# Attention's opening in another order: u first, head copies on ScalarE, both tables at once, the second unit turned in idle banks, diagonals by halves

## The chip, the cores and the metric

The kernel runs on one core of one Trainium2 chip. A core has five engines with an instruction queue each, which run side by side and wait for one another by semaphores: TensorE (PE, matrix products and transposes; its weight loads have a row of their own, PEld), VectorE (DVE), ScalarE (ACT), GpSimd (POOL) and SyncE (SP, which here only issues transfers). Every queue is worked off in order: an instruction that waits holds up all that stand behind it on its engine. Sixteen DMA engines move data between the memory and the core's SBUF. PE writes its results to PSUM[...].

The metric is the device time of one execution in microseconds (us); the time of a kernel is the median of its runs.

## The reference

Two stages follow each other. The first is a linear attention with decay (RWKV-5), for 4 batches, 8 heads, 768 steps and a head size of 48:

```python
for t in range(S):
    kt, vt, rt = (k[:, :, t], v[:, :, t], r[:, :, t])
    cur = np.einsum('bhd,bhe->bhde', u[None] * kt, vt)
    y[:, :, t] = np.einsum('bhd,bhde->bhe', rt, state + cur)
    state = w[None, :, :, None] * state + np.einsum('bhd,bhe->bhde', kt, vt)
```

Each head's state fades by `w` at every step; the step's own product of key and value enters the output with the factor `u` and the state with the factor 1. The output, laid out as 3072 tokens of 384 numbers, goes to the second stage, a mixture of 8 experts. A gate gives a score to every pair of token and expert; the pairs are taken in falling order of score until each expert has exactly 384 tokens, and each token goes through its expert, `relu(x @ w1[e]) @ w2[e]` with 1024 hidden numbers.

## The kernel before

**Units.** The attention (class `Mild`) is cut into 24 units, one for each batch and each chunk of 128 steps, chunk by chunk. Unit n has three loads of 192 KB, k, r and v, which SP issues in the order of need (`load`, L336); a buffer slot for k and r is used again five units later, one for v six units later. `start` issues the loads of k and r of units 0 to 4 and v of units 0 to 3; the loop of unit n issues k and r of unit n+5 and v of unit n+4.

**What is done for a unit.** `again` (L340) copies the first head of the second half (k and r) once more behind the last head, so that every pair of heads that is turned together can be read as 112 neighbouring columns. `turn` transposes k and r on PE, four transposes each (L456, L462), into PSUM tiles kT_ps and rT_ps and scales them on the way out with tables of powers of w: in unit 0 with small pieces of the table Q (L468), in units 1 and 2 with the tables WK and WR (L471, L474); from unit 3 on POOL scales the keys beforehand (`keys`, L431, with the table wk) and ACT copies kT out (L473). `own` computes r·k·u for every step on POOL (L437, L438), `own_sum` sums it by head on DVE into dd (L443), and `diagonal` writes eight matrices AT with dd on the diagonal on ACT (L484). `pairs` multiplies keys and r on PE into g_ps (L494), and DVE lays the upper part of it over AT (L498). `keep` forms the product of keys and values for the state (L511). `outputs` multiplies AT with v on PE (L532), and ACT copies the result x out (L550). `rows` transposes x back (L581), ACT copies it (L588), and SP writes it to memory (L589), from where the experts fetch their tokens.

**The order.** The order on each engine is written out by hand, by the order of the calls in `Mild.run`. In the loop of unit n, `turn` is two units ahead of `outputs` and `pairs` one. Ahead of the loop stands the opening, which the change rewrites:

```python
        self.start()
        self.again(0)
        self.turn(0, "pieces")
        self.own(0)
        self.idle(4, "y_ps")
        self.tables()
        self.wk_table()
        self.again(1)
        self.own_sum(0)
        self.diagonal(0)
        self.turn(1, "tables")
```

`start` also loads w and the row u_row (on ACT's queue, L360), makes the identity matrix, clears buffers, and computes the powers of w on DVE, then Q, half on POOL and half on DVE (L391). `spread_u` spreads u over the partitions by a product with a row of ones (u_ps, L406) and ACT copies it to u_bc (L407). `tables` copies WK and WR out of Q on ACT (L418). `wk_table` transposes WK on PE (L425), and ACT copies the result to wk (L426). `idle` issues transposes of the identity that nobody reads (L412). Inside `turn(0, "pieces")` the u product and three unread transposes stand between k's and r's transposes. u_ps, wk_ps, y_ps and the unread transposes share the PSUM tile with the tag y_ps.

**After the attention.** In the last units, pieces of the expert assignment are run between attention's steps. Then the experts follow one by one: a search for the next expert that fills, the fetch of its tokens by rows (POOL, indirect), its weights (SP), and the products. All of this is tied to attention's results and to the order on the engines, not to a point in time.

## Time and profile before

| | |
|---|---|
| median of 3 runs | 410.83 us (410.79 to 411.12) |
| the profiled execution | 411.54 us, of which the trace spans 409.8 |
| PE busy | 385.9 us |
| DVE, ACT, POOL busy | 274.0, 159.3, 140.5 us |
| PE's first product of unit 0 (L494) | at 15.30 us |
| the same of units 1, 2, 3, 4, 5 | at 18.60, 22.50, 28.05, 32.17, 36.29 us |
| loads k, r, v and writes of x_rows | 192 KB each; 3.0 to 5.3 us from issue to landing in the median |

Times are microseconds from the span's start. In a timeline line the first number is the start, the second the length from the first to the last of the merged instructions, then come engine, line, operation, output and inputs; in brackets stands for how long the engine was idle before it and whose result ended that. A name with q (SPq, ACTq) is the engine's queue, which issues transfers. In a line of the table of stretches the stretch is followed by its length, then by each engine's busy time with its number of instructions, the granted PE clock, the DMA engines' share and the rate.

### The profile page before, as it was taken

Reading aid. Unit: us, or ns where it says so; the run is one execution under the profiler, and the core shown is the slowest. Engines: PE = TensorE matmul, PEld = TensorE weight load, DVE = VectorE, ACT = ScalarE, POOL = GpSimd, SP = SyncE. Lnnn points to the kernel's source line nnn. Section 1 sums busy time; section 2 is a strip of 40 time slices with the busy share of each in tenths; the row PEclk is TensorE's granted clock in tenths of the full one; section 3 lists DMA queues with packets and bytes.
Section 4 is the critical chain, followed back from the end, with each engine's and each line's share of the span. In section 5 each row is a group of like instructions: output and inputs, shape, how many; then the busy total and the mean of one; then the engine's idle time right before and its main releaser. Section 6 shows DMA issues by size and latency. Waiting matters only on the chain.

```text
span 409.8 us, 8707 instructions
## 1 busy us (share of the span) xinstructions
PE 385.9 (94%) x3245; PEld 291.7 (71%) x3245; DVE 274.0 (67%) x951; ACT 159.3 (39%) x413; POOL 140.5 (34%) x172
## 2 busy tenths in 40 slices
PE   5899999999999897899999999999999999999993
PEld 3778888888877564558558757856856956966991
DVE  5776676566886789779487477568658852971630
ACT  1697888788873310222222221221312312132130
POOL 5697878566742021103403203202311222040020
PEclk9999999999999999999999999999999999999998
DMA  9999997988591263009219109108216365180010
GB/s 122 163 155 199 200 172 142 172 155 156 107 354 38 87 234 150 20 2 333 82 22 354 40 19 347 59 19 293 87 44 231 136 208 217 36 332 20 2 59 26
DMA packets 95301, 57.29 MB, mean 140 GB/s; under 512 B 77201, under 2 KB 89490, under 8 KB 95250
## 3 DMA queue, kind: packets, MB, share of 16 engines
q1 hardware_dynamic: 91520, 47.19, 46.5%
q0 software_dynamic: 3072, 9.44, 6.4%
q8 instruction: 27, 0.44, 0.5%
q14 instruction: 24, 0.20, 0.1%
q10 hardware_dynamic: 658, 0.01, 0.1%
HBM read 47.20 MB, written 9.44 MB: 138 GB/s over the span
## 4 chain that ended last, share of the span: by engine, by line
PE 63%; DVE 18%; DMA 11%; ACT 3%; issue 3%; POOLq 0%; ACTq 0%; DVEq 0%
PE h_ps L1494 18%; PE p_ps L1567 9%; DMA out_dram<-o_all,to 9%; PE y_ps L532 7%; PE o_ps L1594 6%; PE g_ps L494 5%; PE kv_ps L511 2%; PE kT_ps L456 2%; PE rT_ps L462 2%; PE x_ps L581 2%; PE lg_ps L561 2%; PE xT_ps L1485 2%; ACT AT L484 1%; DVE H L1545 1%; DMA xg<-x_rows,tok 1%
## 5 line engine op out<-in xcount | busy, mean ns | idle before, releaser
L1494 PE MATMUL h_ps<-xT,w 128*128 128x384 f32 (+1 forms) x384 | 122.5, 469 | 0.7 <-ACT xT L1486 0.6
L1494 PEld LDWEIGHTS h_ps<-xT,w 128*128 128x128 f32 x384 | 65.7, 190 | 37.0 <-issue 3.6
L1496 ACT ACTIVATE hid<-h_ps 128x384 f32<-128x384 f32 (+1 forms) x64 | 29.7, 464 | 93.7 <-PE h_ps L1494 88.4
L1470 POOL DMA_INDIRECT xg<-x_rows,tok x22 | 22.9, 1040 | 112.2 <-issue 69.6
L484 ACT ACTIVATE AT<-ident,dd 128x128 f32<-128x128 f32 x192 | 58.6, 390 | 1.2 <-DVE dd L443 1.2
L1588 POOL DMA_INDIRECT out_dram<-o_all,to x16 | 20.0, 1247 | 75.8 <-DVE o_all L1576 73.7
L498 DVE COPY_PREDICATED AT<-mask,g_ps 128x512 f32<-128x512 uint8 x48 | 32.7, 734 | 12.6 <-PE g_ps L494 12.3
L1571 ACT COPY res<-p_ps 128x384 f32<-128x384 f32 (+2 forms) x28 | 13.2, 473 | 59.0 <-PE p_ps L1567 59.0
L1594 PE MATMUL o_ps<-w,hid 128*128 128x384 f32 x96 | 32.8, 486 | 0.0
L494 PE MATMUL g_ps<-rT,kT 48*128 48x128 f32 x384 | 27.9, 285 | 0.6 <-DVE AT L498 0.6
L431 POOL TENSOR_TENSOR kss<-krs,wk 128x384 f32<-128x384 f32 x24 | 24.3, 1016 | 9.6 <-DVE krs L340 8.1
L494 PEld LDWEIGHTS g_ps<-rT,kT 48*128 48x128 f32 x384 | 23.3, 187 | 3.7 <-PE rT_ps L462 0.9
L438 POOL TENSOR_TENSOR rk<-rk,u_bc 128x384 f32<-128x384 f32 x24 | 24.2, 1008 | 4.6 <-ACT u_bc L407 2.8
L532 PE MATMUL y_ps<-AT,vts 128*64 128x128 f32 x384 | 25.7, 276 | 0.0
L437 POOL TENSOR_TENSOR rk<-krs 128x384 f32<-128x384 f32 x24 | 24.5, 1021 | 0.0
L1594 PEld LDWEIGHTS o_ps<-w,hid 128*128 128x128 f32 x96 | 17.4, 190 | 9.8
L532 PEld LDWEIGHTS y_ps<-AT,vts 128*64 128x64 f32 x384 | 20.6, 137 | 1.0 <-issue 0.3
L1567 PE MATMUL p_ps<-T,S 128*128 128x192 f32 x120 | 20.7, 327 | 0.0
L1545 DVE TENSOR_TENSOR H<-hid 128x512 f32<-128x512 f32 x12 | 7.9, 687 | 19.1 <-ACT hid L1496 19.1
L550 ACT COPY x<-y_ps 128x512 f32<-128x512 f32 x24 | 14.0, 584 | 16.0 <-PE y_ps L532 16.0
L1567 PEld LDWEIGHTS p_ps<-T,S 128*128 128x128 f32 x120 | 19.6, 190 | 0.0
L1567 PEld LDWEIGHTS p_ps<-w,hid 128*128 128x128 f32 x112 | 17.3, 190 | 1.9
(301 smaller groups left out, 691.6 us busy)
## 6 DMA issues: line engine op xcount, KB each, us to landing
w<-in_moe_w_dram SPq DMA_DIRECT2D x18, 1536.0 KB, 7.2
krs<-in_k_dram SPq DMA_DIRECT2D x24, 192.0 KB, 3.9
krs<-in_r_dram SPq DMA_DIRECT2D x24, 192.0 KB, 5.3
vts<-in_v_dram SPq DMA_DIRECT2D x24, 192.0 KB, 5.3
x_rows<-xr SPq DMA_DIRECT2D x24, 192.0 KB, 3.0
xg<-x_rows,tok POOLq DMA_INDIRECT x22, 4.5
out_dram<-o_all,to POOLq DMA_INDIRECT x16, 3.1
out_dram<-o_sb,to POOLq DMA_INDIRECT x5, 2.6
```

The source lines that it names most:

```text
L431: self.nc.gpsimd.tensor_mul(self.kss[:, n % self.NS].rearrange("p (g h) d -> p g h d", g=2)[:, :, :, 0:D], src, self.wk.rearrange("p (g h) ...
L437: nc.gpsimd.tensor_mul(rk, self.krs[:, n % self.NK, 1, 0:H, 0:D], self.krs[:, n % self.NK, 0, 0:H, 0:D])
L438: nc.gpsimd.tensor_mul(rk, rk, self.u_bc)
L484: nc.scalar.mul(AT[:, z, a, :], self.ident, dd[:, h:h + 1])
L494: nc.tensor.matmul(g_ps[:, z, a, :], kT[rows, a, :], rT[rows, a, :], start=True, stop=True)
L498: nc.vector.copy_predicated(out=AT[:, z], mask=self.mask.unsqueeze(1).to_broadcast([128, HP, T]), data=g_ps[:, z])
L532: nc.tensor.matmul(yv[q * PD:(q + 1) * PD, o // 2, o % 2, :], lhsT, rhs, start=(o // 2, q) not in seen, stop=stop, skip_group_check=True)
L1470: nc.gpsimd.indirect_dma_start(out=xg[:, c, :], out_offset=None, in_=x_dram[0:within, :], in_offset=bass.IndirectOffsetOnAxis(ap=tok[:, c: ...
L1494: nc.tensor.matmul(h_ps[:, 0:m], w1[:, f, ts(j, 128)], xT[:, f, 0:m], start=(f == 0), stop=(f == KD - 1))
L1496: nc.scalar.activation(hid[:, j, 0:m], h_ps[:, 0:m], AF.Relu)
L1567: nc.tensor.matmul(ps[:, q, :], left[a][:, j, :], right[b][:, j, :], start=(j == 0), stop=(j == KF // 2 - 1))
L1594: nc.tensor.matmul(o_ps, hid[:, j, ts(c, 128)], w2[:, j, :], start=(j == 0), stop=(j == KF - 1))
```

## The change

The opening's calls are put into another order, and some move to other engines.

- u_row is loaded from POOL's queue instead of ACT's. Its product comes first on PE, after 12 unread transposes instead of 14; the other unread transposes (3 and 4) are gone.
- `again` of units 0, 1 and 2 becomes two copies on ACT each (`again_one`, one for k and one for r), where it was one copy on DVE that waited for both loads. From unit 3 on it stays on DVE.
- k and r of unit 0 are turned one right after the other. Unit 1 is turned before the products of unit 0 as before, but into PSUM tiles of the assignment that stand idle at that time (tags few and counts), with WK's transposes between its k and r.
- WK and WR are made one after the other on ACT with `again_one` of unit 1 between; `chunk` comes later on DVE.
- `diagonal` goes by halves of the heads: all of z = 0, then all of z = 1. In unit 0 the copies for unit 2 stand between and behind the halves.
- `keys(0)` moves ahead of `pairs(0)` in the program.
- Units 3 to 23 and all that follows keep their code; only the order of the eight diagonals within a unit differs.

```diff
--- before.py
+++ after.py
@@ -339,6 +339,10 @@
         kr, HP, H, D = self.krs[:, n % self.NK], self.HP, self.H, self.D
         self.nc.vector.tensor_copy(kr[:, :, H, 0:D], kr[:, :, HP, 0:D])
 
+    def again_one(self, n, x):
+        t, HP, H, D = self.krs[:, n % self.NK, x], self.HP, self.H, self.D
+        self.nc.scalar.copy(t[:, H, 0:D], t[:, HP, 0:D])
+
     def start(self):
         nc, HP, H, D = self.nc, self.HP, self.H, self.D
         half = HP // 2
@@ -357,10 +361,10 @@
         AB = self.ones8
         nc.vector.memset(AB[:, :, :, :, 0:1], 1.0)
         nc.gpsimd.memset(self.wgp, 0.0)
-        nc.scalar.dma_start(self.u_row, self.u.rearrange("h d -> (h d)").unsqueeze(0))
+        nc.gpsimd.dma_start(self.u_row, self.u.rearrange("h d -> (h d)").unsqueeze(0))
         nc.vector.memset(self.one_row, 1.0)
         nc.scalar.copy(self.bad, self.ident[:, 0:HP])
-        self.idle(14, "y_ps")
+        self.idle(12, "g_ps")
 
         nc.gpsimd.memset(self.mask_f, 1.0)
         nc.gpsimd.affine_select(out=self.mask_f, in_=self.mask_f, compare_op=ALU.is_ge, fill=0.0, base=-1,
@@ -401,29 +405,30 @@
                                      self.wg.rearrange("(a z d) e -> z d a e", z=2, d=self.D)[z])
 
     def spread_u(self):
-        nc, H, D = self.nc, self.H, self.D
         u_ps = self.ps.tile([128, 512], F32, name="u_ps", tag="y_ps")
-        nc.tensor.matmul(u_ps[:, 0:H * D], self.one_row, self.u_row, start=True, stop=True)
-        nc.scalar.copy(self.u_bc.rearrange("p h d -> p (h d)"), u_ps[:, 0:H * D])
+        self.nc.tensor.matmul(u_ps[:, 0:self.H * self.D], self.one_row, self.u_row, start=True, stop=True)
+        return u_ps
+
+    def copy_u(self, u_ps):
+        self.nc.scalar.copy(self.u_bc.rearrange("p h d -> p (h d)"), u_ps[:, 0:self.H * self.D])
 
     def idle(self, m, tag):
         ps = self.ps.tile([128, 512], F32, name="unread_ps", tag=tag)
         for _ in range(m):
             self.nc.tensor.transpose(ps[:, 0:T], self.ident, self.ident)
 
-    def tables(self):
-        nc, AB = self.nc, self.ones8
-        for t, x in ((self.WK, "k"), (self.WR, "r")):
-            for at, q in self.pieces[x]:
-                nc.scalar.copy(t[:, :, at], q)
-        nc.vector.tensor_mul(self.chunk, AB[:, 0, :, 1, 8], AB[:, 0, :, 1, 8])
-
-    def wk_table(self):
-        nc, HP, D = self.nc, self.HP, self.D
+    def table(self, t, x):
+        for at, q in self.pieces[x]:
+            self.nc.scalar.copy(t[:, :, at], q)
+
+    def wk_turned(self):
         ps = self.ps.tile([128, 2, 512], F32, name="wk_ps", tag="y_ps")[:, 0].rearrange("p (a s) -> p a s", s=T)
-        for a in range(HP):
-            nc.tensor.transpose(ps[:, a, :], self.WK[:, a, :], self.ident)
-        nc.scalar.copy(self.wk, ps.rearrange("p a (z d) -> p (a z) d", z=2)[:, :, 0:D])
+        for a in range(self.HP):
+            self.nc.tensor.transpose(ps[:, a, :], self.WK[:, a, :], self.ident)
+        return ps
+
+    def wk_table(self, ps):
+        self.nc.scalar.copy(self.wk, ps.rearrange("p a (z d) -> p (a z) d", z=2)[:, :, 0:self.D])
 
     def keys(self, n):
         D = self.D
@@ -447,42 +452,46 @@
         s = 2 * a if t.shape[1] == self.H or 2 * a < self.HP else 2 * a + 1
         return t[:, s:s + 2, :].rearrange("p q d -> p (q d)")[:, 0:PD + self.D]
 
-    def turn(self, n, raw=None):
-        nc, HP, P = self.nc, self.HP, PD + self.D
-        kr = self.krs[:, n % self.NK]
-        key = self.kss[:, n % self.NS] if raw is None else kr[:, 0]
-        kT_ps = self.ps.tile([128, HP, T], F32, name="kT_ps")
-        for a in range(HP):
-            nc.tensor.transpose(kT_ps[0:P, a, :], self.pair(key, a), self.ident)
-        if raw == "pieces":
-            self.spread_u()
-            self.idle(3, "y_ps")
-        rT_ps = self.ps.tile([128, HP, T], F32, name="rT_ps")
-        for a in range(HP):
-            nc.tensor.transpose(rT_ps[0:P, a, :], self.pair(kr[:, 1], a), self.ident)
-        kT = self.pool.tile([128, HP, T], F32, name="kT")
-        rT = self.pool.tile([128, HP, T], F32, name="rT", bufs=3)
-        if raw == "pieces":
-            for t, t_ps, x in ((kT, kT_ps, "k"), (rT, rT_ps, "r")):
-                for at, q in self.pieces[x]:
-                    nc.vector.tensor_mul(t[0:P, :, at], t_ps[0:P, :, at], q[0:P])
+    def turned(self, n, t, pool, name, tag):
+        ps = pool.tile([128, self.HP, T], F32, name=name, tag=tag)
+        for a in range(self.HP):
+            self.nc.tensor.transpose(ps[0:PD + self.D, a, :], self.pair(t, a), self.ident)
+        return ps
+
+    def keys_turned(self, n, raw=False, pool=None, tag="kT_ps"):
+        key = self.krs[:, n % self.NK, 0] if raw else self.kss[:, n % self.NS]
+        return self.turned(n, key, pool or self.ps, "kT_ps", tag)
+
+    def r_turned(self, n, pool=None, tag="rT_ps"):
+        return self.turned(n, self.krs[:, n % self.NK, 1], pool or self.ps, "rT_ps", tag)
+
+    def scaled(self, n, x, ps, how):
+        nc, P = self.nc, PD + self.D
+        t = self.pool.tile([128, self.HP, T], F32, name=x + "T", bufs=2 if x == "k" else 3)
+        if how == "pieces":
+            for at, q in self.pieces[x]:
+                nc.vector.tensor_mul(t[0:P, :, at], ps[0:P, :, at], q[0:P])
+        elif how is None:
+            nc.scalar.copy(t[0:P], ps[0:P])
         else:
-            if raw:
-                nc.vector.tensor_mul(kT[0:P], kT_ps[0:P], self.WK[0:P])
-            else:
-                nc.scalar.copy(kT[0:P], kT_ps[0:P])
-            nc.vector.tensor_mul(rT[0:P], rT_ps[0:P], self.WR[0:P])
-        self.live[n].update(kT=kT, rT=rT)
-
-    def diagonal(self, n):
+            nc.vector.tensor_mul(t[0:P], ps[0:P], how[0:P])
+        self.live[n][x + "T"] = t
+
+    def turn(self, n, raw=False):
+        kT_ps = self.keys_turned(n, raw)
+        rT_ps = self.r_turned(n)
+        self.scaled(n, "k", kT_ps, self.WK if raw else None)
+        self.scaled(n, "r", rT_ps, self.WR)
+
+    def diagonal(self, n, zs=(0, 1)):
         nc, HP = self.nc, self.HP
-        AT = self.pool.tile([128, 2, HP, T], F32, name="AT", bufs=3)
-        dd = self.live[n]["dd"]
-        for a in range(HP):
-            for z in range(2):
+        if "AT" not in self.live[n]:
+            self.live[n]["AT"] = self.pool.tile([128, 2, HP, T], F32, name="AT", bufs=3)
+        AT, dd = self.live[n]["AT"], self.live[n]["dd"]
+        for z in zs:
+            for a in range(HP):
                 h = self.head(a, z)
                 nc.scalar.mul(AT[:, z, a, :], self.ident, dd[:, h:h + 1])
-        self.live[n]["AT"] = AT
 
     def pairs(self, n, between=None):
         nc, HP, D = self.nc, self.HP, self.D
@@ -604,22 +613,37 @@
         N, B, C, walk = self.N, self.B, self.C, self.walk
         self.live = {n: {} for n in range(N)}
         self.start()
-        self.again(0)
-        self.turn(0, "pieces")
+        u_ps = self.spread_u()
+        self.again_one(0, 0)
+        k0 = self.keys_turned(0, True)
+        self.again_one(0, 1)
+        r0 = self.r_turned(0)
+        self.copy_u(u_ps)
         self.own(0)
-        self.idle(4, "y_ps")
-        self.tables()
-        self.wk_table()
-        self.again(1)
+        self.scaled(0, "k", k0, "pieces")
+        self.scaled(0, "r", r0, "pieces")
+        self.table(self.WK, "k")
+        self.again_one(1, 0)
+        self.table(self.WR, "r")
+        self.again_one(1, 1)
+        k1 = self.keys_turned(1, True, walk.ps, "few")
+        wk_ps = self.wk_turned()
+        r1 = self.r_turned(1, walk.ps, "counts")
+        self.wk_table(wk_ps)
+        self.scaled(1, "k", k1, self.WK)
         self.own_sum(0)
-        self.diagonal(0)
-        self.turn(1, "tables")
+        self.diagonal(0, (0,))
+        self.again_one(2, 0)
+        self.diagonal(0, (1,))
+        self.again_one(2, 1)
+        self.scaled(1, "r", r1, self.WR)
         self.own(1)
+        self.keys(0)
         self.own_sum(1)
-        self.again(2)
+        nc, AB = self.nc, self.ones8
+        nc.vector.tensor_mul(self.chunk, AB[:, 0, :, 1, 8], AB[:, 0, :, 1, 8])
         self.pairs(0)
         self.diagonal(1)
-        self.keys(0)
         self.own(2)
         chores = walk.constants()
         for n in range(N):
@@ -628,7 +652,7 @@
             if n == 2:
                 self.gate_weights()
             if n == 0:
-                self.turn(2, "tables")
+                self.turn(2, True)
                 self.again(3)
                 self.own_sum(2)
                 self.pairs(1)
```

## Prediction

> **What bounds the kernel now.** I read the page first, then stretches of the opening, then each engine's timeline from 0 to 42 us, then the loads.
>
> ```profile
> span 409.8 us, 8707 instructions
> PE 385.9 (94%) x3245; PEld 291.7 (71%) x3245; DVE 274.0 (67%) x951; ACT 159.3 (39%) x413; POOL 140.5 (34%) x172
> PE 63%; DVE 18%; DMA 11%; ACT 3%; issue 3%; POOLq 0%; ACTq 0%; DVEq 0%
> ```
>
> PE is busy for 94% and carries most of the chain that ended last. It is idle for 23.9 us in all, so an opening can be worth a few us at most.
>
> ```profile
> 0.00:15.30 15.30, 10.60 (x43) 7.90 (x43) 7.76 (x24) 3.94 (x10) 8.72 (x19) 1.00 1.17 136
> 15.30:28.05 12.75, 11.07 (x145) 9.03 (x144) 10.66 (x21) 11.99 (x39) 10.86 (x12) 1.00 1.20 146
> 28.05:32.17 4.12, 4.12 (x64) 3.63 (x61) 3.09 (x7) 3.91 (x12) 3.84 (x5) 1.00 1.12 198
> ```
>
> The third stretch is one unit of the settled loop: PE has no gap in 4.12 us, and ACT fills 3.91. From 28 us on whatever PE has gained or lost stays. In the second stretch ACT is the full engine (11.99 of 12.75). So the question is where ACT and PE stand when that regime begins.
>
> ```profile
> 8.09 0.46 PE L456 MATMUL kT_ps<-ident,krs 128*112 128x128 f32 x1 [1.91 <-DVE krs L340]
> 8.48 1.64 PE L406 MATMUL u_ps<-u_row,one_row 1*128 1x384 f32 x2
> 15.30 1.16 PE L494 MATMUL g_ps<-rT,kT 48*128 48x128 f32 x16
> 26.91 0.61 PE L581 MATMUL x_ps<-ident,x 112*128 112x112 f32 x4 [0.68 <-ACT x L550]
> ...
> 14.91 4.78 ACT L484 ACTIVATE AT<-ident,dd 128x128 f32<-128x128 f32 x16
> 20.23 2.45 ACT L484 ACTIVATE AT<-ident,dd 128x128 f32<-128x128 f32 x8 [0.54 <-DVE dd L443]
> 26.28 0.58 ACT L550 COPY x<-y_ps 128x512 f32<-128x512 f32 x1
> ...
> 19.54 0.19 DVE L340 COPY krs<-krs 128x96 f32<-128x96 f32 x1
> 19.65 0.54 DVE L443 TENSOR_REDUCE dd<-rk 128x8 f32<-128x384 f32 x1
> ```
>
> Unit 0's fourth key transpose waits for a DVE copy until 8.09, then u's product blocks r's transposes; the first products come at 15.30. ACT starts its diagonals at 14.91 and is full until it ends x of unit 1 at 26.86; PE waits for that until 26.91, and has no wait of this size in the opening afterwards.
>
> ```profile
> krs<-in_r_dram SPq DMA_DIRECT2D x12, 192.0 KB, 5.3
> ...
> 10.71 1.14 SPq L336 DMA_DIRECT2D krs<-in_r_dram  x1
> ```
>
> The loads are a ladder. Issue plus landing of single ones: k0 1.89+3.3 = 5.2, k1 3.15+4.4 = 7.55, r2 7.15+5.3 = 12.45, v2 11.90+5.3 = 17.2, k5 16.86+5.2 = 22.1, r5 18.03+6.1 = 24.1. Between are steps of 1.19 us, so r0 6.4, r1 8.8, k2 11.25, k3 14.8, r3 10.71+5.3 = 16.0, r4 19.6. The DMA engines are full from 3.4 us on, so the ladder stays.
>
> **What the Trainium skill says.** "DMA: Bandwidth & Descriptors", Anatomy of one DMA — SWDGE (gpsimd) path: a transfer issued on GpSimd costs about 2.0 us fixed plus bytes/436e3. Here indirect ones from POOL land 2.6 to 4.7 us after issue, and these count. "SBUF — State Buffer", SBUF: two separate sides: while VectorE runs a two-port operation, GpSimd can't write descriptors. DVE clears krs from 1.25 to 2.64 us, just then; no run here shows the effect. "TensorE: Matmul & The Clock Gate", Part 1: The HAM clock gate: full clock after some 3.4 us of sustained work. The trace agrees: transposes start every 0.22 us until 14.33, then every 0.11, after PE had worked nearly without pause since 10.70. "ScalarE: Activation LUTs", What ACT_TABLE_LOAD costs: 186 ns + 0.833 ns per element; for a head copy of 48 that is 0.23 us (estimate). The trace's 128x32 copy took 0.19.
>
> **The change part by part.** I lay the new order on the measured durations.
>
> *u_row on POOL.* POOL's clears end at 4.42 and Q waits until 6.08 for DVE: 1.65 us of cover. The issue costs POOL 0.95 to 1.93 (the indirect issues), so Q slips by 0 to 0.3; I take 0. Issued at about 1.5, u_row lands at 4.1 to 6.2; I take 4.7. One issue of 0.66 leaves ACT's queue, where a table load follows that ends before k0 lands: nothing. SP's issues stay in their order.
>
> *PE.* Twelve transposes by 0.22 end at 4.2. u's product 4.7 to 6.3 (1.64); k0 turned to 7.4 and r0 to 8.25 (1.06 each); k1 (copy at 8.1) to 9.1, WK to 10.0, r1 to 10.9; products of unit 0 at 10.7 instead of 15.30: 4.6 earlier. PE's instructions after that are the same ones.
>
> *DVE.* Q ends at 7.12 as before; the copy of 1.00 at 7.04 is gone. Scaling k0 7.45 to 8.2, r0 to 9.05, k1 9.2 to 9.85, dd of unit 0 to 10.4 (POOL's rk: 6.7, 8.0, 9.0), r1 to 11.6, dd of unit 1 to 12.15.
>
> *ACT.* Head copies of unit 0 behind k0 (5.2) and r0 (6.4); u_bc 6.7 to 7.2; WK to 7.9, copy, WR to 8.8, copy to 9.05; wk 10.05 to 10.5. Diagonals of unit 0 from 10.45, with the two copies for unit 2 (0.4; k2 11.25 and r2 12.45 have landed): to 13.3. Unit 1: 2.4, to 15.7. So ACT comes to the diagonals of unit 2 at 15.7 instead of 20.23.
>
> *What is late next.* These diagonals need dd of unit 2, and on DVE that stands behind `again(3)`, which waits for both k3 and r3. Before, it ran at 19.54, long after r3; now r3 at 16.0 ends the wait: 16.05+0.2+0.5 = 16.75. ACT stands idle for 1.05. Gain here 20.23-16.8 = 3.4. Then x of unit 0 to 19.75, kT of unit 3 to 20.3; dd of unit 3 is ready at 20.4 (`again(4)` waits for r4 at 19.6): the diagonals run to 22.8 where they ended at 26.0; xr to 23.2; x of unit 1 from 23.1, before 26.28. PE's wait thus ends at 23.75 instead of 26.91: **3.2 us**. PE itself had reached this point earlier: products of unit 2 at 18.1 (pairs of unit 1 leave g_ps at 18.05), y of unit 1 to 21.3, so ACT's date counts.
>
> *Behind it.* `again(5)` waits for r5 at 24.1; dd of unit 4 at 24.85, diagonals 24.9 (before 27.93, gain 3.0), and x of unit 2 lands just in time. DMA stood partly idle from 20 to 24 us (loads waited for a free slot); now k6 can follow at 20.3, r6 lands near 26.8 (needed 27.5), r7 near 31.2 (needed 31.6). I take off 0.1 for these close calls. The other edits (chunk, keys(0), order of diagonals, fewer unread transposes) fall in gaps of DVE, POOL and PE: nothing; keys(0) needs wk at 10.5 and is used only at 17.
>
> Sum: 3.1. The profiled execution took 411.54 for its span of 409.8, so 1.74 lie around it; the median of the runs is 0.7 below. 411.54-3.1 = 408.4 for that execution, 410.83-3.1 = **407.7** as the median.
>
> **Rivals.**
> Smaller gain (0.20): u_row lands past 5.7. The 1.05 us for which ACT waits for r3 cover the first us of lateness, after that each us costs one; or the loads, now without a pause, fall behind by 0.25 us a unit (three loads at 1.19 and a write near 0.8 are 4.4 against 4.12 per unit) over units 5 to 7. Either takes 0.8 to 2: 408.5 to 409.8.
> No gain (0.04): PE stays at half clock past 14.3, because the waits for k2, r2 and the copies break its work up. From 13.9 to 21.3 some 6 us of full-speed work would double and y of unit 1 end at 26, as before: 410.8. Against it: from 6.3 to 12 PE has no long gap.
> Slower (0.10): the POOL load of u_row. PE's whole queue stands behind it. Break-even is a landing at 8.8 us: 4.7, plus 1.05 of cover, plus 3.1 of gain. The krs clear on DVE and the full DMA engines speak for it; against it the slowest landing from POOL seen, 4.7 after issue. At a landing of 10 us: 412.0.
> More gain (0.06): r3 lands 1 us earlier, or DVE gets to the copy otherwise; then ACT's 15.7 counts: 4.2 gain, 406.6.
>
> **How the numbers follow.** The likeliest case has 0.60, with a range of its own of 407.1 to 408.5. A measurement tells 0.2% (0.8 us) from no change. Slower and no gain, 0.14, are left outside the range; it holds the smaller gains to 409.8 and most of the larger ones to 406.6. Faster by over 0.2% 0.86, within 0.2% 0.04, slower 0.10.
>
> **What would show it.** Right: u_ps begins before 5.7; first g_ps near 11; the diagonals of unit 2 start near 16.8, idle before them by DVE's dd, and DVE idle before its copy of unit 3 by a load; x_ps of unit 1 near 23.7; units 3 to 5 g_ps every 4.12 from 24.9. Wrong: u_ps after 6, PE's transposes at 0.22 spacing after 14, or PE waiting for r transposes behind loads in units 6 to 8. If the opening gains 3 us and the time doesn't, the loss lies past 42 us, where I looked at the page only.

## The result, and the profile after

The changed kernel takes 408.76 us (median of 12 runs, 408.59 to 412.16) against 411.15 us (median of 12, 410.79 to 412.11) of the kernel before, measured beside it: a ratio of 0.9957 with a 95% interval of 0.9932 to 0.9981. Faster was forecast, and 407.7 us; it is faster, and by less. Nine of the twelve executions lie between 408.6 and 408.9 us and three at 412.1, with a mean granted TensorE clock of 0.983 to 0.988 against 0.992 to 0.997; the ratio is one of means, so these three are why it says 1.8 us while the medians say 2.4.

The profiled execution took 408.76 us, its span is 406.9. The page of after, its head:

```profile
span 406.9 us, 8688 instructions
PE 383.4 (94%) x3236; PEld 290.0 (71%) x3236; DVE 272.6 (67%) x948; ACT 160.6 (39%) x419; POOL 141.2 (35%) x173
```

PE's share is 94% as before: it was busy for 2.5 us less (among other things nine transposes that nobody reads are gone, 3245 instructions before, 3236 now), and its idle time stayed (23.5 us, before 23.9). This balance names no cause: work that is taken out of a stretch in which PE waits for others doesn't shorten the stretch by itself. The table of stretches of after says more (columns: stretch, length, busy time and number of instructions of PE, PEld, DVE, ACT, POOL, granted PE clock, DMA share, GB/s); the cuts are the first products of unit 0, of unit 3 and of unit 4:

```profile
0.00:10.04 10.04, 7.51 (x34) 5.58 (x34) 6.71 (x21) 4.57 (x13) 8.02 (x18) 0.91 0.99 120
10.04:25.61 15.57, 11.79 (x145) 9.80 (x145) 10.37 (x20) 12.54 (x40) 12.85 (x14) 0.95 1.38 159
25.61:29.85 4.24, 4.24 (x65) 3.61 (x61) 3.17 (x7) 4.03 (x13) 3.60 (x5) 1.00 1.05 210
```

The first stretch is 5.3 us shorter (before 15.30), the second 2.8 us longer (before 12.75): over half of what the opening gains is given back before unit 3. From there on PE has no gap, as before. The timeline of after from 1.6 to 26 us shows where it is given back; in brackets is the idle time before an instruction and whose result ended it:

```profile
4.18 1.21 PE L409 MATMUL u_ps<-u_row,one_row 1*128 1x384 f32 x2
10.04 1.92 PE L503 MATMUL g_ps<-rT,kT 48*128 48x128 f32 x16
24.48 0.60 PE L590 MATMUL x_ps<-ident,x 112*128 112x112 f32 x4 [1.57 <-ACT x L559]
...
12.76 2.44 ACT L494 ACTIVATE AT<-ident,dd 128x128 f32<-128x128 f32 x8
16.91 2.45 ACT L494 ACTIVATE AT<-ident,dd 128x128 f32<-128x128 f32 x8 [1.71 <-DVE dd L448]
21.14 0.99 ACT L494 ACTIVATE AT<-ident,dd 128x128 f32<-128x128 f32 x3 [0.83 <-DVE dd L448]
23.84 0.58 ACT L559 COPY x<-y_ps 128x512 f32<-128x512 f32 x1
24.89 0.59 ACT L475 COPY kT<-kT_ps 112x512 f32<-112x512 f32 x1 [0.47 <-DMA krs<-in_r_dram]
...
16.21 0.21 DVE L340 COPY krs<-krs 128x96 f32<-128x96 f32 x1 [1.35 <-DMA krs<-in_r_dram]
19.82 0.75 DVE L340 COPY krs<-krs 128x96 f32<-128x96 f32 x1 [1.68 <-DMA krs<-in_r_dram]
20.50 0.54 DVE L448 TENSOR_REDUCE dd<-rk 128x8 f32<-128x384 f32 x1
...
1.60 0.70 POOL L364 DMA_DIRECT2D u_row<-in_u_dram  x1
19.51 2.16 POOL L436 TENSOR_TENSOR kss<-krs,wk 128x384 f32<-128x384 f32 x2
```

Read it from below. u_row is issued on POOL at 1.60 us and has landed before PE asks for it at 4.18. ACT is through with the diagonals of unit 1 at 15.20 and then stands for 1.71 us: the sum dd of unit 2 is in DVE's queue behind the head copy of unit 3, which waits for r3 (16.21). One unit on the same happens again: the head copy of unit 4 waits for r4 until 19.82, takes 0.75 us, the sum follows, and ACT's diagonals of unit 3 start at 21.14, after 0.83 us of idling. What PE waits for at 24.48 is ACT's copy x behind these diagonals. Before, that instruction came at 26.91: **2.43 us** are won there, and 2.32 us stand at the products of units 4, 5 and 6 (29.85, 33.97 and 39.67 us, before 32.17, 36.29 and 42.00).

The spans differ by 2.9 us. Of that 2.47 have come about when the last run of products with w1 begins (389.39 us, before 391.86); that run took 5.52 us here and 5.96 in the profiled execution of before, which was itself 0.4 us above the median of its runs. These 0.44 us lie in a run of products whose code is the same, and are not counted as the change's.

### The profile page after: what moved, and what is told of

It is laid out like the page before. It is cut to its first block, busy times and chain, and to the rows that moved or that the text cites. A ratio compares the mean times of both kernels' runs of the same rounds, so it can differ in the third digit from the quotient of the medians.

```text
span 406.9 us, 8688 instructions
## 1 busy us (share of the span) xinstructions
PE 383.4 (94%) x3236; PEld 290.0 (71%) x3236; DVE 272.6 (67%) x948; ACT 160.6 (39%) x419; POOL 141.2 (35%) x173
## 5 line engine op out<-in xcount | busy, mean ns | idle before, releaser
L503 PEld LDWEIGHTS g_ps<-rT,kT 48*128 48x128 f32 x384 | 24.1, 193 | 3.8 <-PE rT_ps L458 1.1
L541 PE MATMUL y_ps<-AT,vts 128*64 128x128 f32 x384 | 25.7, 276 | 0.0
L1591 PEld LDWEIGHTS p_ps<-T,S 128*128 128x128 f32 x120 | 19.6, 190 | 0.0
L477 DVE TENSOR_TENSOR rT<-rT_ps,WR 112x512 f32<-112x512 f32 x23 | 15.8, 685 | 4.4 <-PE rT_ps L458 4.4
```

What stands on the lines that cost most here:

```text
L503: nc.tensor.matmul(g_ps[:, z, a, :], kT[rows, a, :], rT[rows, a, :], start=True, stop=True)
L541: nc.tensor.matmul(yv[q * PD:(q + 1) * PD, o // 2, o % 2, :], lhsT, rhs, start=(o // 2, q) not in seen, stop=stop, skip_group_check=True)
L1591: nc.tensor.matmul(ps[:, q, :], left[a][:, j, :], right[b][:, j, :], start=(j == 0), stop=(j == KF // 2 - 1))
```

## The experiments

The theory was that the ladder of loads sets the date of the settled loop, through DVE's head copies that stand ahead of the sums. Rivals: that u's load, the copies on ACT or PE's own work set it; and that TensorE's clock, not waits, takes the rest of the gain. Each expectation gives its theories letters and says what they mean there. The kernels of one group ran on one chip beside the kernel before (411.4 to 412.3 us there), so ratios are compared, and the dates in the traces. The ratio of the changed kernel itself is 0.9957 and, on two other chips, 0.9967 and 0.9946; its fastest execution lies 2.2 us below the fastest of the kernel before on all three. The changed kernel's own dates are 24.48 us for PE's x of unit 1 and 33.97 us for the products of unit 5.

### The sum ahead of the head copy

```diff
                 self.turn(2, True)
-                self.again(3)
                 self.own_sum(2)
+                self.again(3)
                 self.pairs(1)
...
                 step(n, "first")
+                if n < 3:
+                    self.own_sum(n + 2)
                 if n + 3 < N:
                     self.again(n + 3)
                 if n + 2 < N:
-                    if n + 3 < N:
+                    if 3 <= n < N - 3:
                         self.own_sum(n + 2)
```

> Edit to the changed kernel: for units 2 to 5 own_sum (dd) comes ahead of again on DVE, so dd no longer stands behind the head copy that waits for the r load two ladder steps on. Theory A (the recorded one: ACT's diagonals of units 2 and 3 start by dd, and dd starts by r3 and r4): diagonals of unit 2 at about 15.4 instead of 16.91, of unit 3 at about 20.1 (then set by POOL's rk, ready at 19.55) instead of 21.14; unit 1's x_ps about 23.5 instead of 24.48; time 1.0 us below the changed kernel (407.7 where that has 408.7). Theory B (the opening is set by PE's own work and waits, ACT is only near it): x_ps of unit 1 stays within 0.3 of 24.48 and so does the time.

Measured: 408.67 us, ratio 0.9920 (0.9909 to 0.9932). Timeline of this kernel:

```profile
14.79 0.54 DVE L448 TENSOR_REDUCE dd<-rk 128x8 f32<-128x384 f32 x1
16.12 0.21 DVE L340 COPY krs<-krs 128x96 f32<-128x96 f32 x1 [0.79 <-DMA krs<-in_r_dram]
19.50 0.55 DVE L448 TENSOR_REDUCE dd<-rk 128x8 f32<-128x384 f32 x1 [1.91 <-POOL rk L443]
...
15.37 2.45 ACT L494 ACTIVATE AT<-ident,dd 128x128 f32<-128x128 f32 x8 [0.25 <-DVE dd L448]
20.15 1.86 ACT L494 ACTIVATE AT<-ident,dd 128x128 f32<-128x128 f32 x6 [1.38 <-DVE dd L448]
...
23.49 0.61 PE L590 MATMUL x_ps<-ident,x 112*128 112x112 f32 x4 [0.39 <-ACT x L559]
```

With the sum first, ACT's wait before unit 2's diagonals falls from 1.71 to 0.25 us and they start 1.54 us earlier. The next ones start 1.0 us earlier only, because now the sum waits for POOL's product (19.50), which in turn began after `again(3)`. PE's x of unit 1 comes 1.0 us earlier; of this 0.6 is left at unit 5 (33.36). The fastest execution lies 3.0 us below the fastest of the kernel before, 0.8 more than the changed kernel's. The order of two instructions on DVE thus held back what the change could have given, as theory A expected.

### The ladder itself: k and r ahead of the first v

```diff
-        for n, what in ((0, "kr"), (1, "kr"), (0, "v"), (2, "kr"), (1, "v"), (3, "kr"), (2, "v"), (4, "kr"), (3, "v")):
+        for n, what in ((0, "kr"), (1, "kr"), (2, "kr"), (0, "v"), (3, "kr"), (4, "kr"), (1, "v"), (2, "v"), (3, "v")):
```

> Edit to the changed kernel: only the order of the first loads: v0 behind unit 2's k and r, v1 and v2 behind unit 4's. r3 then lands one ladder step earlier, near 14.8, r4 two steps earlier, near 17.2. Theory A (the ladder of loads sets the opening): the DVE copy of unit 3 moves from 16.21 to about 15.0 and unit 4's from 19.82 to 17.5; diagonals of unit 2 start near 15.7, of unit 3 near 20; the time falls by 1.0 to 1.4 us. Theory B (loads are hidden, the PE and ACT work is what counts): no change, within 0.3 us.

Measured: 408.94 us, ratio 0.9915 (0.9902 to 0.9928). Timeline of this kernel:

```profile
15.16 0.21 DVE L340 COPY krs<-krs 128x96 f32<-128x96 f32 x1 [0.32 <-DMA krs<-in_r_dram]
17.57 1.01 DVE L340 COPY krs<-krs 128x96 f32<-128x96 f32 x1 [0.47 <-DMA krs<-in_r_dram]
24.34 0.21 DVE L340 COPY krs<-krs 128x96 f32<-128x96 f32 x1 [3.11 <-DMA krs<-in_r_dram]
...
17.51 1.00 POOL L443 TENSOR_TENSOR rk<-rk,u_bc 128x384 f32<-128x384 f32 x1
...
24.27 0.33 ACTq L404 DMA_DIRECT2D wgp<-in_moe_w_gate_dram  x1
24.65 0.59 ACT L475 COPY kT<-kT_ps 112x512 f32<-112x512 f32 x1 [2.16 <-DMA krs<-in_r_dram]
...
22.54 0.60 PE L590 MATMUL x_ps<-ident,x 112*128 112x112 f32 x4 [0.67 <-ACT x L559]
28.47 0.60 PE L590 MATMUL x_ps<-ident,x 112*128 112x112 f32 x4 [1.59 <-ACT x L559]
```

Earlier loads of r3 and r4 bring PE's x of unit 1 to 22.54 us, 1.9 us ahead of the changed kernel. Then 1.7 of it are lost again in one unit: x of unit 2 waits until 28.47 us, and unit 5 comes at 33.72, 0.25 us ahead. Two things stand before it. DVE's copy of unit 5 waits until 24.34 us for r5, which has hardly moved (24.59 in the changed kernel), and the sum of unit 4 behind it is ready at 25.02. And ACT's queue holds the second load of the gate weights (24.27), which by the profile goes out only when r5 has landed; ACT's next copy behind it comes after 2.16 us of idling, and the diagonals of unit 4 start at 25.50. So beyond the late sum the gate weights can have cost 0.5 us at most; the larger part is r5's. This trace is of the longest of the five executions (409.13 us). The fastest lies 3.1 us below the fastest of the kernel before, where the changed kernel's lies 2.2 below, so over the whole kernel the reordered ladder is worth some 0.9 us more, near what theory A expected, and the 0.25 us of this one trace understate it.

### The head copies back on DVE

```diff
-        self.again_one(0, 0)
+        self.again(0)
...
-        self.again_one(0, 1)
...
-        self.again_one(1, 0)
...
-        self.again_one(1, 1)
+        self.again(1)
...
-        self.again_one(2, 0)
...
-        self.again_one(2, 1)
...
+        self.again(2)
         self.pairs(0)
```

> Edit to the changed kernel: the head copies of units 0, 1 and 2 go back to DVE as one copy each that waits for both loads; all else stays. Theory A: the first products are later by 1 to 2.5 us (11 to 12.5 instead of 10.04), but ACT's 1.71 us of waiting for dd of unit 2 absorbs it: diagonals of unit 2 within 0.4 of 16.91, time within 0.4 us of the changed kernel. Theory C (the gain is the sum of the waits removed, the copy's 1.9 on PE among them): time 1.5 to 2 us worse than the changed kernel.

Measured: 411.04 us, ratio 0.9977 (0.9966 to 0.9988). Timeline of this kernel:

```profile
8.44 0.46 PE L458 MATMUL kT_ps<-ident,krs 128*112 128x128 f32 x1 [1.79 <-DVE krs L340]
13.65 2.08 PE L503 MATMUL g_ps<-rT,kT 48*128 48x128 f32 x16
...
7.38 1.01 DVE L340 COPY krs<-krs 128x96 f32<-128x96 f32 x1
10.47 1.03 DVE L340 COPY krs<-krs 128x96 f32<-128x96 f32 x1
...
10.44 0.99 POOL L443 TENSOR_TENSOR rk<-rk,u_bc 128x384 f32<-128x384 f32 x1
```

The first products come at 13.65 us instead of 10.04, and unit 5's at 35.04: 1.07 us later. So 2.5 of the 3.6 us were hidden by ACT's waits for the ladder, and 1.07 were not: more than the 0.4 us that theory A allowed and less than the 1.5 that theory C asked for, so neither was right and the ladder is not all that counts. PE waits for copies which take 1.0 us on DVE, where ACT's took 0.23; a copy that begins at 10.47 ends at 11.50, just behind POOL's product (10.44 to 11.43).

### u's load late

```diff
-        nc.gpsimd.dma_start(self.u_row, self.u.rearrange("h d -> (h d)").unsqueeze(0))
         nc.vector.memset(self.one_row, 1.0)
...
         nc.gpsimd.memset(self.states, 0.0)
+        nc.gpsimd.dma_start(self.u_row, self.u.rearrange("h d -> (h d)").unsqueeze(0))
```

> Edit to the changed kernel: the load of u_row is issued on POOL behind the clears of kss, vts and states, about 2.5 us later (near 4.1 instead of 1.6), with PE's queue behind it. Theory A: u_ps starts near 6.7 instead of 4.18, first products 1 to 1.7 later; ACT's wait of 1.71 for dd of unit 2 shrinks to below 0.5 and covers nearly all of it: time within 0.4 us of the changed kernel. Theory C (u first on PE is itself the gain, each us of lateness costs one): time 1.5 to 2.5 us worse.

Measured: 410.59 us, ratio 0.9964 (0.9951 to 0.9977). Timeline of this kernel:

```profile
8.15 1.61 PE L409 MATMUL u_ps<-u_row,one_row 1*128 1x384 f32 x2 [3.90 <-DMA u_row<-in_u_dram]
...
16.34 4.97 ACT L494 ACTIVATE AT<-ident,dd 128x128 f32<-128x128 f32 x16
...
4.13 0.71 POOL L374 DMA_DIRECT2D u_row<-in_u_dram  x1
```

The transfer of 1.5 KB took 4.0 us from issue to PE's start, while the DMA engines moved 180 GB/s; issued at 1.60, when they moved 46, it landed after 2.2. A landing at 8.1 was later than I had expected. u's product came 4.0 us late, and unit 5's products 0.95 us late (34.92). That is more than the 0.4 us of theory A and less than the 1.5 of theory C. (The ratio doesn't show it, because none of the five executions is a long one; the fastest lies 1.2 us below the fastest of the kernel before, the changed kernel's 2.2, so the loss is about 1.0 us there too.) The other 3 us were covered: ACT's waits of 1.71, 0.83 and 0.47 us in the changed kernel, 3.0 together, are all gone here, and units 1 and 2 follow each other without a gap (16.34). It is still 1.4 us ahead of the kernel before. So the cover is three times as long as the 1.05 us that the prediction gave it, and the landing that breaks even lies beyond the 8.8 us named there: near 9.5 us, an estimate from 8.15 and the 1.37 us left at unit 5, if every further us costs one.

### The changed kernel again

No edit; one group later, on another chip.

> The changed kernel once more, unaltered, beside the next three on one chip. All theories: 2.3 us less at unit 5's products than before (33.97 against 36.29) and so about 2.3 us less time in most executions; some executions near 3.4 us above those, at a lower granted PE clock, if the clock theory (D) holds.

Measured: 410.22 us, 22 runs from 408.55 to 412.46, ratio 0.9967 (0.9953 to 0.9981). Its profiled execution, 410.34 us, is one of the longer ones. Its table of stretches:

```profile
26.00:28.00 2.00, 2.00 (x24) 1.78 (x22) 0.88 (x3) 2.00 (x7) 1.92 (x2) 0.60 1.31 206
28.00:30.00 2.00, 2.00 (x18) 1.67 (x15) 1.20 (x4) 0.61 (x2) 1.17 (x3) 0.55 1.20 208
```

The same stretches in the changed kernel's first profile:

```profile
26.00:28.00 2.00, 2.00 (x33) 1.71 (x32) 1.24 (x3) 2.00 (x8) 1.92 (x2) 1.00 0.98 213
28.00:30.00 2.00, 2.00 (x30) 1.66 (x30) 1.58 (x5) 1.79 (x5) 1.44 (x2) 1.00 1.14 211
```

Up to 25.7 us the dates of PE's products g_ps agree within 0.1 us in the two executions. Then PE is granted half its clock for some 3.4 us, does 42 instructions in 4 us where it did 63, and unit 5's products come at 35.50 instead of 33.97. One such stretch costs 1.5 us here. The changed kernel's first profile has one of the same length too, from 8.25 to 11.66 us (the 0.91 and 0.95 in its table of stretches): unit 0's products took 1.92 us there and 1.16 here, but unit 1's products, which wait for DVE in both, came at 13.84 and 13.85. Where the stretch falls decides what it costs, so the mean clock of an execution is no measure of its time. "TensorE: Matmul & The Clock Gate", HAM oscillation — how this bites in real kernels, in the Trainium skill describes a clock that falls after waits and the work behind it starting at half speed; the trace has PE waiting for 1.6 us at 16.0 and again at 23.0, and busy for 6.8 of the 10 us from 16 to 26. The first profile has the same two waits (1.53 and 1.57 us) and no fall behind them.

### PE's waits filled

```diff
         self.again_one(0, 1)
+        self.idle(4, "g_ps")
         r0 = self.r_turned(0)
+        self.idle(4, "g_ps")
...
                 self.own_sum(2)
+                self.idle(4, "y_ps")
                 self.pairs(1)
...
+                    if n == 1:
+                        self.idle(10, "kT_ps")
                     self.turn(n + 2)
+                if n == 2:
+                    self.idle(10, "counts", walk.ps)
```

(`idle` gets a pool as a further argument.)

> Edit to the changed kernel: unread transposes of the identity fill PE's waits: 4 ahead of unit 0's r, 4 behind it, 4 ahead of unit 1's products, 10 ahead of unit 3's keys, 10 ahead of unit 1's x_ps. Theory D (the executions near 412 have PE at half clock over one or two stretches because the new order leaves PE gaps of 0.5 to 1.6 us): none of this kernel's executions lies more than 1.5 us above its fastest, and the fastest are within 0.3 us of the changed kernel's. Theory E (they come from elsewhere, the clock is only a sign): as large a share of slow executions as the changed kernel has beside it.

Measured: 409.39 us, ratio 0.9952 (0.9936 to 0.9967); six runs from 409.17 to 410.38, clock 0.994 to 0.997. The slowest execution is 1.21 us above the fastest, while the changed kernel's 22 on the same chip reach 3.9 above theirs. But the fastest is 0.6 us slower than the changed kernel's fastest, since the added transposes delay work (unit 5 at 34.54). So theory D is right on the steadiness and wrong on the cost. Six runs are few, but the other kernels speak for it as well. In those whose traces show both waits of about 1.5 us, near 16 and 23 us (the changed kernel and the last two experiments below), 29 of 70 executions lie more than 1.5 us above their kernel's fastest; where at most one of the two is left (this kernel, the sum first, the ladder, u's load late, and the combined kernel below) it is 2 of 34. Against it: the kernel with the copies on DVE has 7 of 22 such executions, at mean clocks of 0.994 to 0.998, and the longest of the kernel before have as high a clock, so there is a second source that is not this one. That the waits cause the fall of the clock is made likely by this, not shown.

### Sum first, ladder, and gate weights on SP

The edits of the first two experiments together, and:

```diff
-            self.nc.scalar.dma_start(self.wgp[z * PD:z * PD + self.D, :, 0:self.E],
+            self.nc.sync.dma_start(self.wgp[z * PD:z * PD + self.D, :, 0:self.E],
```

> Edit to the changed kernel: dd ahead of again for units 2 to 5 (as in sum_first), the first loads of v later (as in v_later), and the two loads of the gate weights issued on SP instead of ACT. Theory A with a lane wait (in v_later ACT stood 2.16 us in its queue behind the second gate-weight load, until r5 landed, and gave back what the ladder had won): that wait is gone; diagonals of unit 2 at 15.3, of unit 3 near 19.1, x_ps of unit 1 near 22.5 and of unit 2 below 27.5 (28.47 in v_later); then again of unit 6 waits for r6 near 28 and ends the gain: unit 5's products near 33.2, time 0.6 to 1.0 below the changed kernel. Theory B (waits on loads don't set it): no better than sum_first alone.

Measured: 407.50 us (407.27 to 408.79), ratio 0.9907 (0.9890 to 0.9924); the changed kernel beside it 410.22. Once more on a third chip:

> The kernel called three once more, on another chip, beside the changed kernel. Theory A: its fastest executions lie 1.2 to 1.4 us below those of the changed kernel (products of unit 5 at 32.7 against 33.97 us), ratio to the kernel before 0.989 to 0.992. Rival: its lead came from the chip; less than 0.7 us below.

Measured: 407.99 us, ratio 0.9917 (0.9899 to 0.9934), one of six runs 2.2 us above the fastest. The changed kernel beside it:

> The changed kernel unaltered, beside the next three on the same chip. Theory A (opening gains 2.3 us; in some executions TensorE falls back to half speed for one stretch near 27 to 30 us): fastest executions 2.2 to 2.7 us below the fastest of the kernel before, some 1.5 us or more above its own fastest. Rival (the gain itself is unsteady): fastest executions less than 2 us below.

Measured: 409.34 us (409.03 to 411.21), ratio 0.9946 (0.9928 to 0.9964); four of six runs within 0.6 us of the fastest, two 1.6 and 2.2 above it. The fastest executions of the combined kernel are 1.28 us below those of the changed kernel on the one chip and 1.38 on the other. Timeline of the combined kernel (its first profile):

```profile
22.61 0.60 PE L590 MATMUL x_ps<-ident,x 112*128 112x112 f32 x4 [0.67 <-ACT x L559]
26.79 0.55 PE L590 MATMUL x_ps<-ident,x 112*128 112x112 f32 x4
31.60 0.60 PE L590 MATMUL x_ps<-ident,x 112*128 112x112 f32 x4 [0.53 <-ACT x L559]
32.73 1.16 PE L503 MATMUL g_ps<-rT,kT 48*128 48x128 f32 x16
```

x of unit 2, which waited until 28.47 us in the ladder experiment, comes at 26.79 without a wait: the sum behind r5 and the gate weights together were what gave its gain back. No run has the ladder with only one of the two. Unit 5 comes at 32.73, 1.24 us ahead of the changed kernel. The last wait, of unit 3 at 31.60, goes back to the next rung (DVE's copy of unit 6 waits for r6 until 27.93). This version beats both kernels; the opening had another 1.3 us in it that the change left.

### The head copy behind the pairs

On top of the combined kernel, for units 3 to 10:

```diff
-                self.again(3)
                 self.pairs(1)
+                self.again(3)
...
-                if n + 3 < N:
+                if n > 7 and n + 3 < N:
                     self.again(n + 3)
...
                     self.pairs(n + 1, lambda: step(n, "products"))
+                if n <= 7:
+                    self.again(n + 3)
```

> Edit to the kernel three: for units 3 to 10 the head copy on DVE also goes behind the masked copies of pairs, so that nothing but the keys of that unit waits for its r. Theory A: unit 5's products near 32.3, time another 0.5 to 1.0 below three. If the DMA engines are the bound by then (three loads and a write per unit), the wait only moves to PE's r transposes and the time stays within 0.3 of three.

Measured: 418.38 to 425.73 us in six runs, ratio 1.0221 (1.0177 to 1.0265, without the longest): by the ratios 13 us slower than the combined kernel, and neither expectation was near it. Timeline of this kernel:

```profile
23.72 0.65 PE L458 MATMUL kT_ps<-ident,kss 128*112 128x128 f32 x4 [1.59 <-POOL kss L436]
29.68 0.66 PE L458 MATMUL kT_ps<-ident,kss 128*112 128x128 f32 x4 [1.77 <-POOL kss L436]
...
22.66 1.01 POOL L436 TENSOR_TENSOR kss<-krs,wk 128x384 f32<-128x384 f32 x1 [1.89 <-DVE krs L340]
```

I had looked at who waits for the sum and not at who waits for the copy. POOL's scaled keys read the copied head, and PE's transposes of the next unit read the scaled keys. With the copy moved behind the pairs, that path closes into a loop longer than 4.12 us: up to 61 us PE waits for scaled keys in seven of eight units, 10.7 us in all.

### The gate weights alone on SP

The diff is the one shown with the combined kernel, on the changed kernel.

> The changed kernel with the gate weights' two loads on SP's queue instead of ACT's. Theory A: ACT's wait of 0.47 us before the key copy of unit 3 goes (or falls under 0.2), but PE is busy without a gap from 24.48 us and the diagonals of unit 4 still wait for DVE's sum behind r5 (24.59 us), so the products of unit 5 stay at 33.8 to 34.0 us and the time within 0.3 us of the changed kernel's. Rival: the wait is on the path, unit 5's products come near 33.5 and the time falls by 0.4.

Measured: 409.81 us (22 runs from 409.02), ratio 0.9964 (0.9949 to 0.9978); the changed kernel beside it 409.34, fastest 409.03. Timeline of this kernel:

```profile
24.34 0.59 ACT L475 COPY kT<-kT_ps 112x512 f32<-112x512 f32 x1
...
24.05 0.73 DVE L340 COPY krs<-krs 128x96 f32<-128x96 f32 x1 [0.86 <-DMA krs<-in_r_dram]
...
23.69 1.01 POOL L436 TENSOR_TENSOR kss<-krs,wk 128x384 f32<-128x384 f32 x1
...
33.88 1.16 PE L503 MATMUL g_ps<-rT,kT 48*128 48x128 f32 x16
```

ACT's 0.47 us of waiting are gone, and unit 5's products come 0.09 us earlier. In the changed kernel at most 0.1 us of that wait lay on the path, though it looks just like the longer one in the ladder experiment. As theory A expected.

### The copy of unit 4 in two halves

```diff
+        if n == 4:
+            for x in range(2):
+                self.nc.vector.tensor_copy(kr[:, x, H, 0:D], kr[:, x, HP, 0:D])
+        else:
+            self.nc.vector.tensor_copy(kr[:, :, H, 0:D], kr[:, :, HP, 0:D])
-        self.nc.vector.tensor_copy(kr[:, :, H, 0:D], kr[:, :, HP, 0:D])
```

> The changed kernel with DVE's head copy of unit 4 as two copies, one for k and one for r, so that only half of it stands behind the load of r. Theory A (the 0.75 us of that copy, taken as 0.2, is the mis-sized step): the half behind the load takes 0.2 to 0.4, the diagonals of unit 3 start at 20.6 to 20.9 us (21.14 before), TensorE's x of unit 1 at 24.0 to 24.25 (24.48) and the products of unit 5 at 33.5 to 33.75 (33.97). Rival (the length comes from GpSimd running beside and not from the work): the half takes 0.75 as well, diagonals at 21.1 or later, nothing gained.

Measured: 409.61 us (409.04 to 413.56), ratio 0.9953 (0.9935 to 0.9970); the diagonals of unit 3 start at 21.11, PE's x of unit 1 at 24.45. Timeline of this kernel:

```profile
18.48 0.19 DVE L342 COPY krs<-krs 128x48 f32<-128x48 f32 x1 [0.42 <-DMA krs<-in_k_dram]
19.69 0.86 DVE L342 COPY krs<-krs 128x48 f32<-128x48 f32 x1 [1.01 <-DMA krs<-in_r_dram]
...
19.49 1.98 POOL L440 TENSOR_TENSOR kss<-krs,wk 128x384 f32<-128x384 f32 x2
```

Half the work took longer, 0.86 us, and nothing was gained: the rival holds. The length is not the copy's own. The two copies do the same amount of work; the one at 18.48 started at the same time as one of POOL's products and took 0.19, the one at 19.69 began 0.2 us into POOL's scaled keys and ended at 20.55, when the first of these two instructions (1.98 us together) was ending. (The profiled execution is one with TensorE's half speed from 26.0 to 29.4 us and in two later stretches, which is why it took 413.56; the dates read here lie before them.)

## Why the prediction was right, and where it was too high

**u_row on POOL** was right: landing forecast at 4.7 us, in fact before 4.18; the issue cost POOL 0.70 us, and Q, forecast to slip by 0 to 0.3 and taken as 0, slipped by 0.33. POOL was idle for 1.12 us before it, so DVE's powers of w were late. But they were late by way of POOL: the issue pushed POOL's clear of `states` from 3.23 to 4.10, and DVE's first step on the powers ran into it. Timeline of after:

```profile
4.60 0.47 DVE L389 TENSOR_SCALAR ones<-wp 128x4 f32<-128x4 f32 x1 [1.79 <-DMA wp<-in_w_dram]
...
4.10 0.95 POOL L374 MEMSET states<- 128x1024 f32 x1
```

The step took 0.17 us before, and 0.17 again with u's load late, where the clear is over at 4.18. In three other traces of this opening it begins at 4.51, 4.70 and 4.80 us and takes 0.57, 0.37 and 0.27: it always ends at 5.07 or 5.08, just behind the clear. A short issue on POOL thus delayed DVE, in the way that is told below for the head copy.

**PE's opening** was right, and a little too cautious: first products at 10.04 us, 10.7 forecast. Unit 1's keys were turned by 8.2 us instead of 9.1, since three of their four transposes don't wait for the copied head. That u's product took 1.21 us instead of 1.64 is not the reason: in two other traces of this kernel it took 1.64, and the first products came at 9.97 and 9.63. Behind them PE was late: unit 2's products came at 19.17, 18.1 forecast, after a wait of 1.53 us for the scaled keys of unit 3, which stand behind the same r3. The prediction had not counted that path; it cost nothing, because PE stood waiting for x of unit 1 until 24.48 in any case.

**ACT up to unit 2, and what is late next**: the step that matters held. The diagonals of unit 2 were to start at 16.8 after waiting behind `again(3)` for r3; they started at 16.91, with the wait named. (ACT was not quite full before: it idled for 0.54 us ahead of these diagonals, as the line in the prediction shows.) The experiment with the sum first shows that it was this order.

**The step that was mis-sized** is the next: "dd of unit 3 is ready at 20.4", with `again(4)` "for r4 at 19.6" and a copy of 0.2. r4's copy began at 19.82, 0.22 us later, and took 0.75, 0.55 us longer; the diagonals started at 21.14 and PE's wait ended at 24.48 instead of 23.75. These 0.73 us are the difference between 3.2 and 2.43. The mechanism was right, a term of the sum was not: the copy. The kernel before had shown one of 1.00 us at 7.04, which I took as an exception, and more of 0.35 to 0.50 behind it. What lengthened it was POOL: it met the scaled keys that POOL had begun at 19.51, and ended when the first of these two products did. "SBUF — State Buffer", SBUF: two separate sides, in the Trainium skill, a section that the prediction uses for u_row alone, says that VectorE in a two-port mode and GpSimd share one port pair as an exclusive lock for a whole instruction, with the later one fully blocked. That this copy runs in such a mode no run here shows; but for the rest the traces agree: copies that met a running POOL product ended just behind it, at 18.58 us (product until 18.51) in the ladder experiment, 11.50 (11.43) with the copies on DVE, 24.78 (24.70) with the gate weights on SP, and 8.04 (7.97) in the kernel before. Those that found POOL idle took 0.18 to 0.22 us.

**Behind it**, 24.9 us for the diagonals of unit 4 became 25.74, from the same 0.7 and from the gate weights' load in ACT's queue, which I had not seen; r5 itself ended DVE's wait at 24.59, 24.1 forecast. The loads behind it did not fall behind: DVE waits for a load of r three times in the whole kernel, all before 25 us. The 0.1 us taken off for close calls is what was lost between 2.43 us at x of unit 1 and 2.32 at unit 4; in the trace with the gate weights on SP it is not lost.

**The median.** 2.43 us at unit 1's x and 2.32 from unit 4 on match the 2.39 between the medians. The mean gain is smaller, 0.9957 being 1.8 us, by the three executions at 412.1. No trace of these three was kept; the two profiled executions of this kernel that took 410.3 and 410.6 us each have one half-speed stretch at 26 us.

**Rivals.** The result lies in the range of the "smaller gain" (408.5 to 409.8), but not by its mechanisms: u_row was in time, the loads too. It lies outside the 407.1 to 408.5 us of the likeliest case, so that it lies in the stated range at all is owed to a rival that did not happen, which is luck. "More gain" fell with the wait for r3. "Slower" was priced too high: u's load at 8.1 us still left 1.4 us of gain, because ACT's later waits cover lateness as well as the first. "No gain" had the right mechanism at the wrong place and with the wrong weight: the clock rose as forecast before 14 us, but in some executions it falls at 26 us and takes 1.5 of the 2.4 us back. I had looked for it only where PE was cold to begin with, and not behind the two waits that my own dates left to PE.

## What to carry to other kernels

When an engine is made faster, follow the in-order queue of the one that feeds it to the first instruction that waits for a transfer, and ask what stands behind it for no reason of its own; here two swapped calls and a reordered ladder, with the gate weights' loads moved off ACT's queue, were worth another 1.3 us. Before swapping, list everyone who reads either result: the same copy, moved one step too far, cost 13 us. And take a duration that is five times its median in one row as a message about what ran beside it.

## What the runs showed of the hardware

- A VectorE copy of 128x96 (f32, SBUF to SBUF) takes 0.18 to 0.22 us alone and up to 1.03 beside a GpSimd product, and ends 0.05 to 0.10 us behind that product; halving it changed nothing. A VectorE step of 128x4 behind a GpSimd clear did the same (0.17 us alone, 0.27 to 0.57 behind it). ScalarE's 128x48 copy took 0.22 to 0.23 us beside the same products.
- TensorE's granted clock falls to half for about 3.4 us in some executions of the same program and not in others, after waits that are the same in both: 1.5 us for each at 26 us, nothing at 8 us. In the 413.56 us execution it happened three times, near 26, 135 and 197 us (4.5 us over the fastest), so it is not only the opening's. Why one execution has it and the next has not stays open.
- The load of 1.5 KB issued on GpSimd landed after 2.2 us with DMA engines that moved 46 GB/s, and held PE for 4.0 us from its issue with engines that moved 180.
- A DMA issue in ScalarE's queue stood until a load of SP's queue had landed and held ScalarE for 2.16 us in one kernel and 0.47 in another, by the profile; issued on SP, the wait was gone.
